# Attention weights and results turned by DVE in 32x32 blocks, with the values' products on 16 TensorE tiles

## The chip, the cores and the metric

The kernel runs on one core of a Trainium2 chip. The metric is the time of one execution on the device, in microseconds (us); lower is better. Five engines run their own instruction streams and meet through semaphores: PE (TensorE), DVE (VectorE), ACT (ScalarE), POOL (GpSimd) and SP, which here only issues DMAs. PE's weight loads are listed apart as PEld.

## The reference

The kernel computes an attention over chunks, and feeds its result to a mixture of experts:

```python
batch, n_heads, seq, head_dim = (4, 8, 768, 64)
chunk, left_ctx, right_ctx = (32, 16, 8)          # and 8 memory keys
for c in range(seq // chunk):
    q_c = q[:, :, c_start:c_end]
    k_full = concat([mem_k, k[:, :, l_start:r_end]], axis=2)
    v_full = concat([mem_v, v[:, :, l_start:r_end]], axis=2)
    scores = scale * q_c @ k_full.T
    scores = scores - max(scores, axis=-1)
    a = exp(scores); a = a / (sum(a, axis=-1) + 1e-09)
    out[:, :, c_start:c_end] = a @ v_full
x = out.transpose(0, 2, 1, 3).reshape(3072, 512)

logits = x @ w_gate; P = exp(logits - logits.max())
for _ in range(8):
    P /= P.sum(1) + 1e-09; P /= P.sum(0) + 1e-09; P *= N / E
out = sum(P[:, e:e+1] * (relu(x @ w1[e]) @ w2[e]) for e in range(8))   # w1: 512x1024, w2: 1024x512
```

All tensors are float32.

## The kernel before, in words

**Tiles.** The 3072 tokens are 24 blocks of 128 queries (four chunks of 32 in a block). A chunk sees a window of 64 keys: 8 of memory, 16 to the left, its own 32 and 8 to the right. Four blocks make a unit of 512 tokens. There are 6 units and 8 experts, 48 pairs of them in all. An expert's two products are done in fp16 parts (a high and a low half, three passes) with a scheme of seven block products in the place of eight (`product`, L1591 to L1598); units 0 and 1 begin with plain products (`first_hidden` L2021, `plain_output` L2110) while their other operands are being made.

**Order.** Each piece of work is a task with an engine, a cost, a due time and its dependencies. A planner, `Plan` (L91), runs a small model of the engines when the kernel is built, and from it writes the order of instructions of each engine by hand. A task on SP or ACT that issues DMAs costs 0.5 us for each issue it is said to have. A task marked `many` (scores and values products) is kept 3.6 us from the last such one. Where PE has nothing to do in the early part, `fill` (L424) puts in products on an idle tile ("warm"). A PE task that writes PSUM takes a bank from a named group, and the task that reads it last gives it back. `Plan.run` takes the bank of the group that has been free longest.

**PSUM before.** There are eight banks of 2 KB for each partition. Group `main` (products of the experts, bank 2 at the start), `early` (banks 0 and 1 of an earlier pool, under number 7, for the scores and values of block 1), `att` (3, 4, 5) and `two` (a tile two banks wide, for scores and values products). When block 1 is through, `hand_over` (L1167) gives banks 0 and 1 to `main`; `lent` (L2206) lends one of `att` to `main`; `turn` (L2221) gives all the rest to `main`, when the attention is over.

**Attention.** `load_block` (L832) and `load_values` (L862) issue the DMAs of q, k and v. `transposed` (L993) turns q and k on PE (tiles tq, tk), `scores` (L1049) makes the weights `s`, 128 queries by 8 heads by 64 keys, and `values` (L1112) ends a block:

1. PE turns the weights with four 128x128 transposes through the identity (`go_t`, L1127, tile ta), and ACT copies them out of PSUM (L1146).
2. PE does 32 products, one for each pair of heads, chunk and head of the pair (`go`, L1137, tile xp): keys of a window (64 rows) by queries of a chunk (32 columns), 65 columns wide, the last of ones for the sum. The profile lists each float32 product as two records, so 64.
3. DVE divides by the sum (`share`, L1155 to L1157).
4. PE turns the result back to features by tokens with four transposes (`go_x`, L1178, tile xt), and ACT copies it to `xg` (L1184).

**Loads of the experts.** `load` (L536) fetches a quarter of w1 (two DMAs of 256 KB, L549) or of w2 (one of 512 KB) on the queue of SP. Pieces called w1fm and w2fm are for the steady part ("m"), w1f and w2f for plain products and for the first units. A maximum over each piece (`most`, L558) leads to a power of two by which `split` (L513, L521) scales it into halves. The gate's weights come by one DMA on SP (L2184), and `logits` (L1388, products at L1399) needs them. A second use of room: v of blocks 4 and on, up to block 6, lies in a buffer that the operands of the experts take later (`x_room`).

## Time and profile before

| | |
|---|---|
| median of 3 runs | 1920.35 us (1920.1 to 1921.62) |
| span of the profiled execution, first to last instruction | 1917.9 us |
| the profiled execution's own time | not listed apart; the span lies 2.45 us below the median of the runs |
| busy: PE, PEld, DVE, ACT, POOL | 1903.2, 1641.0, 1436.4, 1033.6, 524.4 us |
| granted TensorE clock, mean | 1.000 |
| PE transposes of weights (L1127, 96 records) and of results (L1178, 96) | 14.6 and 14.5 us busy |
| values products (L1137, 1536 records in three groups) | 21.2 us busy |

A group of instructions is named by its line, engine, operation, output and inputs. PE's records overlap, as matmuls are pipelined, so that a group's busy time can be longer than the time that it adds; the time from the start of one group to the start of the next is the better measure. "Idle before" is the time in which the engine stood still just before a group, and behind the arrow stands what ended that: an instruction, a DMA, or "issue", for which the profile shows no cause.

### The profile page before, as it was taken

What the parts mean: (1) busy time and instruction counts of PE and PEld (TensorE: products, weight loads), DVE (VectorE), ACT (ScalarE), POOL (GpSimd) and SP (SyncE); (2) the same over time, 40 slices, a digit from 0 to 9 for tenths busy, and PEclk for the clock granted to TensorE, in tenths of its full rate; (3) what the DMA queues carried; (4) which work ended last, traced back from release to release, by engine and by line L of the source; (5) the groups of instructions that cost most, each with busy time, mean ns of one, the idle gap of its engine ahead of it and who ended that gap; (6) DMA issues with size and microseconds to landing.
All of it is one profiled execution on the core that took longest, in us unless ns stands there. A gap on an engine that the chain in (4) does not pass through costs nothing.

```text
span 1917.9 us, 47295 instructions
## 1 busy us (share of the span) xinstructions
PE 1903.2 (99%) x19616; PEld 1641.0 (86%) x19616; DVE 1436.4 (75%) x2396; ACT 1033.6 (54%) x2019; POOL 524.4 (27%) x549
## 2 busy tenths in 40 slices
PE   9999999999999999999999999999999999999999
PEld 7777676688888888888888888888888888888888
DVE  6776569778679866898668875898678885786565
ACT  4765565556456545646445554655555554564453
POOL 1220001544224221432124231342124232332112
PEclk9999999999999999999999999999999999999999
DMA  8678753453235342265214533245313732322321
GB/s 198 174 194 209 171 172 116 129 204 125 83 110 172 127 148 85 78 197 185 92 63 149 197 105 127 78 160 176 138 45 105 242 122 94 100 83 84 127 83 67
DMA packets 246791, 254.82 MB, mean 133 GB/s; under 512 B 113264, under 2 KB 180272, under 8 KB 242224
## 3 DMA queue, kind: packets, MB, share of 16 engines
q1 hardware_dynamic: 244452, 251.21, 41.2%
q8 instruction: 153, 2.51, 0.6%
q10 hardware_dynamic: 2124, 0.59, 0.2%
q14 instruction: 62, 0.51, 0.1%
HBM read 187.84 MB, written 63.44 MB: 131 GB/s over the span
## 4 chain that ended last, share of the span: by engine, by line
PE 96%; DMA 2%; DVE 1%; ACT 0%; issue 0%; SPq 0%; ACTq 0%; DVEq 0%
PE px L1598 26%; PE yx L1598 23%; PE pz L1598 13%; PE yz L1598 11%; PE py L1598 6%; PE yp L2126 6%; PE yy L1598 6%; DMA q<-in_q_dram 1%; PE xp L1137 1%; PE sp L1069 1%; PE pp L2045 1%; PE tq L1006 1%; PE tk L1010 0%; PE ta L1127 0%; PE xt L1178 0%; DVE w L521 0%
## 5 line engine op out<-in xcount | busy, mean ns | idle before, releaser
L1598 PEld LDWEIGHTS <-w 128*128 128x128 f16 x7896 | 771.4, 98 | 91.9 <-issue 0.6
L1598 PEld LDWEIGHTS <-h 128*128 128x128 f16 x7056 | 690.4, 98 | 81.4 <-issue 1.5
L1598 PE MATMUL px<-x,w 128*128 128x256 f16 x4512 | 549.1, 273 | 0.0
L1931 POOL TENSOR_TENSOR acc<-acc,y 128x256 f32<-128x256 f32 x252 | 267.5, 1068 | 862.1 <-ACT y L1906 842.7
L1598 PE MATMUL yx<-w,h 128*128 128x256 f16 x4032 | 467.5, 273 | 1.3 <-DVE acc L1941 1.3
L1657 ACT ACTIVATE q<-px 128x256 f32<-128x256 f32 x376 | 142.8, 381 | 294.2 <-PE px L1598 289.5
L1598 PE MATMUL pz<-x,w 128*128 128x256 f16 x2256 | 278.2, 273 | 0.0
L1598 PE MATMUL yz<-w,h 128*128 128x256 f16 x2016 | 233.8, 273 | 0.0
L1826 DVE TENSOR_TENSOR h<-ss,h 128x1024 f16<-128x1024 f32 x160 | 215.0, 1346 | 4.0 <-ACT h L1802 3.5
L1777 ACT ACTIVATE h<-c 128x768 f16<-128x768 f32 x168 | 140.8, 838 | 106.4 <-DVE c L1667 106.4
L1802 ACT CAST h<-ss 128x1024 f16<-128x1024 f32 x168 | 174.1, 1039 | 20.4 <-DVE ss L1766 19.6
L1766 DVE SCALAR_TENSOR_TENSOR ss<-c,ss 128x256 f32<-128x256 f32 x336 | 168.3, 501 | 8.2
L1810 DVE SCALAR_TENSOR_TENSOR h<-c,h 128x768 f16<-128x768 f32 x168 | 165.3, 984 | 9.2 <-ACT h L1777 9.1
L1667 DVE SCALAR_TENSOR_TENSOR c<-px,q 128x256 f32<-128x256 f32 x188 | 78.0, 422 | 103.2 <-PE px L1598 94.9
L1906 ACT ACTIVATE y<-yx,pscale 128x256 f32<-128x256 f32 x168 | 79.4, 473 | 114.8 <-PE yx L1598 110.6
L1598 PE MATMUL py<-x,w 128*128 128x256 f16 x1128 | 139.2, 273 | 0.0
L2126 PE MATMUL yp<-w,h 128*128 128x512 f16 x576 | 132.0, 379 | 0.0
L1667 DVE SCALAR_TENSOR_TENSOR c<-py,q 128x256 f32<-128x256 f32 x188 | 78.5, 422 | 60.2 <-PE py L1598 56.7
L1766 DVE SCALAR_TENSOR_TENSOR ss<-c,h 128x512 f32<-128x512 f32 x168 | 120.8, 719 | 3.1 <-ACT h L1754 3.0
L1598 PE MATMUL yy<-w,h 128*128 128x256 f16 x1008 | 116.9, 273 | 0.0
L2126 PEld LDWEIGHTS <-h 128*128 128x128 f16 x576 | 56.0, 98 | 57.9
L513 ACT ACTIVATE w<-ws,sw 128x1024 f16<-128x1024 f32 (+1 forms) x64 | 69.3, 1089 | 65.5 <-POOL ws L602 65.5
(158 smaller groups left out, 1773.0 us busy)
## 6 DMA issues: line engine op xcount, KB each, us to landing
x<-xkeep SPq DMA_DIRECT2D x28, 1792.0 KB
akeep<-acc SPq DMA_DIRECT2D x168, 256.0 KB
acc<-akeep SPq DMA_DIRECT2D x168, 256.0 KB
w1f<-in_moe_w_dram SPq DMA_DIRECT2D x72, 256.0 KB
w2f<-in_moe_w_dram SPq DMA_DIRECT2D x32, 512.0 KB
w1fm<-in_moe_w_dram SPq DMA_DIRECT2D x56, 256.0 KB
w2fm<-in_moe_w_dram SPq DMA_DIRECT2D x28, 512.0 KB
xkeep<-x SPq DMA_DIRECT2D x6, 1792.0 KB
```

Source lines behind the costliest of these rows:

```text
L513: lambda: nc.scalar.activation(dst(0), src(), AF.Copy, scale=s),
L1598: nc.tensor.matmul(dst.t, a, b, start=(not more and n == 0), stop=(n == end), skip_group_check=more,)
L1657: lambda: nc.scalar.activation(t.t, src.t, AF.Copy, scale=DOWN),
L1667: lambda: nc.vector.scalar_tensor_tensor(c.t[:, o], src.t, DOWN, q.t, op0=ALU.mult, op1=ALU.add),
L1766: lambda: nc.vector.scalar_tensor_tensor(dst(), src(), 0.0, other(), op0=ALU.max, op1=op),
L1777: lambda: nc.scalar.activation(h.t[:, 0, 0:3], c.t, AF.Relu),
L1802: lambda: nc.scalar.copy(h.t[:, 0, 3:7], ss.t),
L1810: lambda: nc.vector.scalar_tensor_tensor(h.t[:, 1, 0:3].rearrange("p a n -> p (a n)"), c.t.rearrange("p a n -> p (a n)"), 0.0, h.t[:, 0, 0 ...
L1826: lambda: spare.tensor_tensor(h.t[:, 1, 3:7], ss.t, h.t[:, 0, 3:7], op=ALU.subtract),
L1906: (lambda: nc.scalar.activation(t.t, src.t, AF.Copy, scale=f))
L1931: lambda: nc.gpsimd.tensor_tensor(acc.t[:, cols], acc.t[:, cols], q.t, op=ALU.add),
L2126: nc.tensor.matmul(py.t, hf.t[:, hl, where[fh], o : o + P], room(fp, WIDE * wl + DM * fh, WIDE * wl + DM * (fh + 1)), start=(fp == 0 and i ...
```

## The change

The values path of a block becomes: DVE turns the weights in 32x32 blocks (`turn_weights`, one instruction of 128x512), PE does 64 products with 32 keys by 32 queries on the 16 tiles of 32x32 that the array divides into, adding up the two halves of a window (`kh`) in PSUM, DVE divides, and DVE turns the result in 32x32 blocks (`turn_out`, two instructions of 128x256). The four transposes on PE at either side and ACT's two copies are gone. A row group of the array is a chunk and writes into a bank of its own, so that the values products take four adjacent banks (before: two).

Blocks of 32x32 leave the features of x in another order over the partitions: the partition group is the pair `w` of heads, and the four tiles of features are (head of the pair, half of the head). The rows of w1 and of the gate follow that order. So a w1 piece that isn't "m" becomes 8 DMAs of 64 KB (before 2 of 256 KB) and the gate 4 DMAs. v lies with a chunk as a group of 32 partitions and the two halves of its window side by side; the memory rows come by 4 DMAs for a batch element instead of 2 and 2 copies, those of blocks 0 and 1 on ACT's queue.

All of PSUM is one tile, and the planner keeps a time for each bank. A task takes the lowest-numbered bank, or run of adjacent banks, that is free (`room`), where before it took the one that had been free longest. `main` begins with bank 0 and `att` with 1 to 7; `hand_over` gives 1 and 2 to `main`, `lent` gives 3. The planner's cost of the values products (0.9) and the distance of `many` tasks stay.

```diff
+    def room(self, takes, now):
+
+        if takes is None:
+            return now, ()
+        banks = self.free[takes.group]
+        best = None
+        for b in sorted(banks):
+            run = takes.only if takes.only is not None else range(b, b + takes.wide)
+            if all(r in banks for r in run):
+                at = max([now] + [banks[r] for r in run])
+                if best is None or at < best[0]:
+                    best = at, tuple(run)
+        return best
...
-                _, bank = heappop(self.free[t.takes.group])
-                t.takes.bank = bank
-                t.takes.made = t.takes.make(bank)
+                banks = self.room(t.takes, at)[1]
+                for b in banks:
+                    del self.free[t.takes.group][b]
+                t.takes.bank = banks
+                t.takes.made = t.takes.make(banks[0])
...
-                    heappush(self.free[b.group], (b.end, b.bank))
+                    self.free[b.group].update((k, b.end) for k in b.bank)
...
-    plan.free["main"] = [(0.0, 2)]
-    plan.free["early"] = [(0.0, 7)]
-    plan.free["att"] = [(0.0, b) for b in range(3, 6)]
-    plan.free["two"] = [(0.0, 6)]
-
+    plan.free["main"] = {0: 0.0}
+    plan.free["att"] = {b: 0.0 for b in range(1, 8)}
...
+    sums = ps.tile([P, 8, 512], F32, name="sums")
+
+    def bank(group, shape, name, wide=1):
+
+        def view(b):
+            if wide > 1:
+                return sums[:, b : b + wide]
+            size = 1
+            for m in shape[1:]:
+                size *= m
+            t = sums[0 : shape[0], b, 0:size]
+            return t if len(shape) == 2 else t.rearrange("p (a b) -> p a b", b=shape[2])
+
+        return Bank(group, view, wide)
...
+    w1g = w1.rearrange("e (g kt p) (fh fp f) -> e fp g p kt fh f", p=CH, kt=KT, fh=2, fp=FP)
...
-            if which == 1:
+            if which == 1 and ahead == "m":
                 for fh in range(2):
                     queue.dma_start(st.t[:, fh], w1v[e, fp, :, :, fh])
+            elif which == 1:
+                for g in range(CB):
+                    for fh in range(2):
+                        queue.dma_start(
+                            st.t[g * CH : (g + 1) * CH, fh], w1g[e, fp, g, :, :, fh]
+                        )
             else:
                 queue.dma_start(st.t, w2v[e, fp])
 
-        return st, add(eng, 2 if which == 1 else 1, go, after, prio, [st], dma=2.1)
+        return st, add(eng, (2 if ahead == "m" else 6) if which == 1 else 1, go, after, prio, [st], dma=2.1)
...
+            for c in range(CB):
+                p0 = c * CH + WIN - CH
                 queue.dma_start(
-                    vt.t[p0 : p0 + NM, 0, :, 0:D], mem_v[b, par::2].rearrange("h m d -> m h d")
-                )
-
-        def copy_m():
-            for par in range(2):
-                p0 = par * KW + WIN
-                src = vt.t[p0 : p0 + NM, 0:1].rearrange("p c h d -> p c (h d)")
-                queue.dma_start(
-                    vt.t[p0 : p0 + NM, 1:CB].rearrange("p c h d -> p c (h d)"),
-                    src.broadcast_to([NM, CB - 1, HP * DV]),
-                )
-
-        def copy_m0():
-
-            for par in range(2):
-                p0 = par * KW + WIN
-                rows = v_pair[p0 : p0 + NM].rearrange("p n c h d -> p (n c) (h d)")
-                nc.scalar.dma_start(
-                    rows[:, 1:], rows[:, 0:1].broadcast_to([NM, 2 * CB - 1, HP * DV])
+                    vt.t[p0 : p0 + NM, 1, :, 0:D], mem_v[b].rearrange("h m d -> m h d")
...
-        def go_v(pars, queue):
-            for par in pars:
-                p0 = par * KW
+        def go_v(halves_, queue):
+            for kh in halves_:
 
                 def part(c, r, t, m):
-
-                    queue.dma_start(
-                        vt.t[p0 + r : p0 + r + m, c, :, 0:D],
-                        v[b, par::2, t : t + m].rearrange("h t d -> t h d"),
-                    )
+                    p0 = c * CH + r
+                    queue.dma_start(vt.t[p0 : p0 + m, kh, :, 0:D], rows(v, b, t, m))
 
                 for c in range(CB):
+                    t = t0 + c * CH - LC
                     if first and c == 0:
-                        part(0, 0, 0, LC)
-                        part(0, LC, 0, CH + RC)
-                    elif last and c == CB - 1:
-                        part(c, 0, S - CH - LC, CH + LC)
-                        part(c, CH + LC, S - RC, RC)
+                        if kh == 0:
+                            part(c, 0, 0, LC)
+                            part(c, LC, 0, CH - LC)
+                        else:
+                            part(c, 0, CH - LC, WIN - CH)
+                    elif last and c == CB - 1 and kh == 1:
+                        part(c, 0, S - LC, LC)
+                        part(c, LC, S - RC, RC)
                     else:
-                        part(c, 0, t0 + c * CH - LC, WIN)
+                        part(c, 0, t + kh * CH, (CH, WIN - CH)[kh])
...
-            if n == 1:
-                lv.append(vs[0][1][-1])
-            else:
-                eng, queue = ("ACT", nc.scalar) if n == 0 else ("SP", nc.sync)
-                lv.append(add(eng, 2, go_m, (), at - 0.1, [vt], dma=0.1))
-                more = [fill_ones] if n == EARLY - 1 else []
-                copy = copy_m if n > 0 else copy_m0
-                lv.append(add(eng, 2, copy, [lv[-1]] + more, at + 0.1, [vt], dma=0.3))
+            eng, queue = ("ACT", nc.scalar) if n < 2 else ("SP", nc.sync)
+            lv.append(add(eng, 4, go_m, (), at - 0.1, [vt], dma=0.2))
...
-        sp = bank("early" if n == 1 else "two", [P, 2, 512], f"sp_{n}")
+        sp = bank("att", [P, 2, 512], f"sp_{n}", 2)
...
-        aT = buf("at", att, [P, HP, QB], F32, f"at_{n}")
-        tp = bank("att", [P, HP, QB], f"ta_{n}")
-        xp = bank("early" if n == 1 else "two", [P, 2, 512], f"xp_{n}")
-        tx = bank("att", [P, HP, QB], f"xt_{n}")
+        aT = buf("at", att, [P, H, 2, CH], F32, f"at_{n}")
+        xp = bank("att", [P, 4, 512], f"xp_{n}", 4)
         g, o = divmod(n * QB, GT)
         if g not in halves:
             halves[g] = (buf("g", att, [P, KT, GT], F32, f"xg_{g}"), [])
         gt = halves[g][0]
 
-        def go_t():
-            for i in range(HP):
-                nc.tensor.transpose(
-                    tp.t[:, i], s.t[:, 2 * i : 2 * i + 2].rearrange("p h d -> p (h d)"), ident
-                )
+        def turn_weights():
+            nc.vector.transpose(
+                aT.t.rearrange("p h k q -> p (h k q)"), s.t.rearrange("p h k -> p (h k)")
+            )
 
         def go():
-            for i in range(HP):
-                for c in range(CB):
-                    cs = slice(c * CH, (c + 1) * CH)
-                    for par in range(2):
-                        r = slice(par * D, (par + 1) * D)
-                        nc.tensor.matmul(
-                            xp.t[cs, par, i * DV : (i + 1) * DV],
-                            aT.t[r, i, cs],
-                            vt.t[r, c, i],
-                            start=True,
-                            stop=True,
-                        )
-
-        t = add("PE", 0.5, go_t, [made], at, [s, aT], takes=tp)
-        t = add("ACT", 0.6, lambda: nc.scalar.copy(aT.t, tp.t), [t], at, [aT], frees=tp)
+            for a in range(2):
+                for kh in range(2):
+                    for c in range(CB):
+                        r = slice(c * CH, (c + 1) * CH)
+                        for w in range(CB):
+                            nc.tensor.matmul(
+                                xp.t[w * CH : (w + 1) * CH, c, a * DV : (a + 1) * DV],
+                                aT.t[r, 2 * w + a, kh],
+                                vt.t[r, kh, 2 * w + a],
+                                start=(kh == 0),
+                                stop=(kh == 1),
+                            )
+
+        t = add("DVE", 0.62, turn_weights, [made], at, [s, aT])
...
         t = add("PE", 0.9, go, [t] + lv, at + 2, [vt, aT], takes=xp, many=n > 1)
         after_v.append(t)
-        xq = buf("at", att, [P, HP, 2, D], F32, f"xq_{n}")
+        xq = buf("at", att, [P, 2, CB, 2, CH], F32, f"xq_{n}")
         rec = buf("sm", att, [P, H], F32, f"rec_{n}")
 
         def share():
-            x = xp.t[:, :, 0 : HP * DV].rearrange("p a (i d) -> p a i d", d=DV)
-            r = rec.t.rearrange("p (a i) -> p a i", a=2)
+            x = xp.t[:, :, 0 : 2 * DV].rearrange("p c (a d) -> p a c d", d=DV)
...
+            pair = Bank("att", lambda b: None, 2, (1, 2))
+
+            def hand_over():
+
+                pair.group = "main"
+
+            add("-", 0.0, hand_over, [t], -2000.0, takes=pair, frees=pair)
+
+        def turn_out():
+            to = gt.t[:, :, o : o + QB].rearrange("p (a k) (c q) -> p a c k q", a=2, c=CB)
+            for a in range(2):
+                nc.vector.transpose(to[:, a], xq.t[:, a])
+
+        t = add("DVE", 0.72, turn_out, [t], at + 2, [xq, gt])
...
-        lambda: nc.sync.dma_start(
-            gate[:, :, 0:E], w_gate.rearrange("(kt p) e -> p kt e", p=P)
-        ),
+        lambda: [
+            nc.sync.dma_start(
+                gate[g * CH : (g + 1) * CH, :, 0:E],
+                w_gate.rearrange("(g kt p) e -> g p kt e", p=CH, kt=KT)[g],
+            )
+            for g in range(CB)
+        ],
...
-            lent = Bank("att", lambda b: None)
+            lent = Bank("att", lambda b: None, 1, (3,))
...
-                for group in ("att", "two"):
-                    for b in plan.free[group]:
-                        heappush(plan.free["main"], b)
-                    plan.free[group] = []
+                plan.free["main"].update(plan.free["att"])
+                plan.free["att"] = {}
```

More of the change, by code (lines that the diff above doesn't have):

```diff
@@ L80, with __init__ @@
 class Bank:
-    def __init__(self, group, make):
+    def __init__(self, group, make, wide=1, only=None):
         self.group, self.make, self.left, self.end, self.made = group, make, 0, 0.0, None
+        self.wide, self.only = wide, only
     @property
@@ L128, in pad @@
         for banks in self.free.values():
-            if banks and banks[0][0] <= now + 0.2:
-                n = int((at - now - 0.1) * 0.8 / 0.11)
-                if n > 0:
-                    _, bank = heappop(banks)
-                    self.fill(bank, n)
-                    heappush(banks, (now + 0.11 * n + 0.2, bank))
-                return
+            for bank, free in banks.items():
+                if free <= now + 0.2:
+                    n = int((at - now - 0.1) * 0.8 / 0.11)
+                    if n > 0:
+                        self.fill(bank, n)
+                        banks[bank] = now + 0.11 * n + 0.2
+                    return
+    def room(self, takes, now):
[10 more added lines that the diff above has]
+        return best
     def next(self, now, w, a, spread):
@@ L142, in next @@
                 continue
-            if t.takes is None or self.free.get(t.takes.group):
-                at = now
-                if t.takes is not None:
-                    at = max(at, self.free[t.takes.group][0][0])
+            room = self.room(t.takes, now)
+            if room is not None:
+                at = room[0]
                 if pick is None or at < pick[0]:
@@ L155, in next @@
                 break
-            if t.takes is None or self.free.get(t.takes.group):
-                at = r
-                if t.takes is not None:
-                    at = max(at, self.free[t.takes.group][0][0])
+            room = self.room(t.takes, r)
+            if room is not None:
+                at = room[0]
                 if pick is None or at < pick[0]:
@@ L302, in tile_chunked_attn_sinkhorn_moe @@
     ps = ctx.enter_context(tc.tile_pool(name="ps", bufs=1, space=PSUM))
-    pstack = ExitStack()
-    early = pstack.enter_context(tc.tile_pool(name="early", bufs=1, space=PSUM))
     astack = ExitStack()
@@ L413, in sums_buf @@
         )
-    def bank(group, shape, name):
-        return Bank(group, lambda b: banks(b).tile(shape, F32, tag=f"b{b}", name=name))
-    def banks(b):
-        return early if b == 7 else late["ps"] if b < 2 else ps
+    sums = ps.tile([P, 8, 512], F32, name="sums")
[9 more added lines that the diff above has]
+        return Bank(group, view, wide)
     FIRM = 200.0
@@ L424, in fill @@
     def fill(b, n):
-        wp = banks(b).tile([P, 256], F32, tag=f"b{b}", name="warm")
         for _ in range(n):
-            nc.tensor.matmul(wp, idle[:, 0:P], idle, start=True, stop=True)
+            nc.tensor.matmul(sums[:, b, 0:256], idle[:, 0:P], idle, start=True, stop=True)
     plan.fill = fill
@@ L1165, in values @@
         if n == 1:
-            def hand_over(t=t):
-                pstack.close()
-                late["ps"] = ctx.enter_context(tc.tile_pool(name="pl", bufs=1, space=PSUM))
-                del plan.free["early"]
-                for b in range(2):
-                    heappush(plan.free["main"], (t.end + 0.2, b))
-            add("-", 0.0, hand_over, [t], -2000.0, takes=Bank("early", lambda b: None))
-        def go_x():
-            for i in range(HP):
-                nc.tensor.transpose(tx.t[:, i], xq.t[:, i].rearrange("p a d -> p (a d)"), ident)
-        t = add("PE", 0.5, go_x, [t], at + 2, [xq, gt], takes=tx)
-        t = add(
-            "ACT",
-            0.6,
-            lambda: nc.scalar.copy(gt.t[:, :, o : o + QB], tx.t),
-            [t],
-            at + 2,
-            [gt],
-            frees=tx,
-        )
+            pair = Bank("att", lambda b: None, 2, (1, 2))
[7 more added lines that the diff above has]
+        t = add("DVE", 0.72, turn_out, [t], at + 2, [xq, gt])
         halves[g][1].append(t)
```

22 lines of the change are left out of this document (10 added, 12 removed).

## The prediction

> **What bounds the kernel now.** I read the page first, then a table by stage, then the PE timeline around one block's values, then the queue of SP and the chain's steps in the first 110 us.
>
> ```profile
> span 1917.9 us, 47295 instructions
> PE 1903.2 (99%) x19616; PEld 1641.0 (86%) x19616; DVE 1436.4 (75%) x2396; ACT 1033.6 (54%) x2019; POOL 524.4 (27%) x549
> q8 instruction: 153, 2.51, 0.6%
> PE 96%; DMA 2%; DVE 1%; ACT 0%; issue 0%; SPq 0%; ACTq 0%; DVEq 0%
> ```
>
> PE is busy for 99% of the span and holds 96% of the chain that ended last: a microsecond of PE work taken out where PE never runs dry is a microsecond of the end. The table by stage says where that is (columns: the stretch, its length, then busy time and count of PE, PEld, DVE, ACT, POOL, then clock, DMA share and GB/s).
>
> ```profile
> 0.00:34.00 34.00, 30.04 (x470) 24.40 (x471) 17.36 (x36) 14.71 (x26) 4.95 (x12) 1.00 0.82 182
> 34.00:110.00 76.00, 72.71 (x1386) 53.66 (x1387) 59.65 (x102) 54.84 (x108) 19.00 (x24) 1.00 0.73 186
> 110.00:290.00 180.00, 177.07 (x3129) 131.31 (x3128) 113.11 (x222) 102.94 (x214) 14.13 (x19) 1.00 0.71 185
> 290.00:400.00 110.00, 109.96 (x777) 75.60 (x775) 91.41 (x176) 62.66 (x116) 45.15 (x44) 1.00 0.46 152
> ```
>
> The attention lies in the first three stretches. From 110 us on PE is the limit (177.07 of 180, and the clock is 1.00). Before 34 us PE's 30.04 us say little, since most of it is filler; from 34 to 110 us PE is nearly full, but its work arrives by a chain of loads. So the change is two changes: PE work taken out of 16 blocks behind 110 us, and more DMA issues on SP in front of it.
>
> **What the change does on PE.** This is the values path of one block in the steady part (start, length, then the group):
>
> ```profile
> 190.79 0.60 PE L1127 MATMUL ta<-ident,s 128*128 128x128 f32 x4
> 191.23 0.82 PE L1598 MATMUL px<-x,w 128*128 128x256 f16 x6
> 191.88 0.82 PE L1598 MATMUL pz<-x,w 128*128 128x256 f16 x6
> 192.63 0.86 PE L1137 MATMUL xp<-v_pair,at 64*32 64x65 f32 x64
> 193.42 0.83 PE L1598 MATMUL pz<-x,w 128*128 128x256 f16 x6
> ...
> 195.40 0.60 PE L1178 MATMUL xt<-ident,xq 128*128 128x128 f32 x4
> 195.83 0.38 PE L1598 MATMUL pz<-x,w 128*128 128x256 f16 x2
> ```
>
> The lengths overlap, since matmuls are pipelined; what a group costs is its start to the next group's start. The weights' transposes (L1127) cost 191.23 − 190.79 = 0.44 us, the results' (L1178) 195.83 − 195.40 = 0.43, the products (L1137) 193.42 − 192.63 = 0.79. The diff removes both groups of transposes, 0.87 us of PE for each block, and certainly does so: no rival has to be made of that.
>
> The products stay the same in multiplications, but in another shape: 64 records on 8 tiles of 64x32 become 128 records on 16 tiles of 32x32, each tile still working through 4 pairs of records. No row shows 16 tiles. Lower bound: 0.79 us, if the tiles set the time, since each has as many pairs as before. Upper bound: 128 × 0.79/64 = 1.58 us, if each record costs PE's sequencer what it costs now. I take 1.06, a third of the way up: 64 records in 0.79 us leave about 12 ns each, the tiles rather than the issue look like the limit, but the number of records and of weight loads doubles, to 256 PE instructions in one task. So 1.06 − 0.79 = +0.27, and 0.87 − 0.27 = 0.60 us saved in a block. Blocks 8 to 23 lie behind 110 us: 16 × 0.60 = **−9.6 us**. The 4.8 us of blocks 0 to 7 fall where loads set the end, and are counted there.
>
> The Trainium skill's page "TensorE: Matmul & The Clock Gate", section "Part 3: Packing small matmuls", gives a pack of 16 tiles as the time of one matmul plus about 4 ns for each further tile. By it the 128 records need some 0.5 us of issue (an estimate from that page), less than the tiles' 0.79, and the term would be 16 × −0.87 = −13.9; no run here shows 16 tiles.
>
> **What moves to DVE and off ACT.**
>
> ```profile
> L1157 DVE TENSOR_TENSOR xq<-xp,rec 128x512 f32<-128x512 f32 x24 | 16.6, 692 | 2.0
> L1290 DVE TENSOR_TENSOR xt<-xs,xs 128x256 f32<-128x256 f32 x2 | 0.8, 424 | 0.2 <-DMA xs<-gkeep 0.2
> L1146 ACT COPY at<-ta 128x512 f32<-128x512 f32 x24 | 14.0, 584 | 6.5 <-PE ta L1127 6.2
> L1184 ACT COPY xg<-xt 128x512 f32<-128x512 f32 x24 | 14.0, 585 | 21.3 <-PE xt L1178 21.1
> ```
>
> No row shows a DVE transpose. By element operations of the same shapes it is 0.69 for the weights and 2 × 0.42 for the results, 1.53 us a block and 37 us in all; ACT loses 2 × 0.585 = 1.17 a block. DVE is busy 59.65 of 76 and 113.11 of 180, so its 1.53 every 9 us or so is covered by PE's own products: 0. If the transposes took twice that, DVE would still have room in the third stretch; in the first it costs at most 1.5 us, and as little as −1.2 if ACT was what held a block. One block's way from weights to x gets shorter: a turn on DVE and one hop less on either side, 2 × (0.60 + 0.58) − 1.53 − 0.27 = about 0.6 us.
>
> **What moves on SP.** Each of the 36 w1 loads by L549 becomes 8 DMAs of 64 KB instead of 2, and the gate 4 instead of 1.
>
> ```profile
> 15.94 5.81 SPq L549 DMA_DIRECT2D w1f<-in_moe_w_dram  x8
> 24.08 5.50 SPq L921 DMA_DIRECT2D w<-in_v_dram  x8
> 57.79 0.39 SPq L2184 DMA_DIRECT2D gate<-in_moe_w_gate_dram  x1
> 75.70 0.94 SPq L549 DMA_DIRECT2D w1f<-in_moe_w_dram  x2
> ```
>
> The first four pieces take 8 issues and 5.81 us: 0.73 each, more than the 0.39 of a free issue, since the engines' queues are full. With 32 issues of smaller DMAs I take 0.40 each: 12.8 us, +7.0 (bounds: 32 × 0.39 = +6.7, 32 × 0.47 = +9.2, by the later w1 row). Behind them on SP stand q, k and v of the next blocks; the 8 v issues at 24.08 took 0.69 each and can fall to 0.40, as their data has the extra time to drain: 8 × 0.29 = 2.3 back. So SP is +4.7 late at 30 us. The first products need all of it:
>
> ```profile
> 26.36 1.21 DVE L558 TENSOR_REDUCE mxs<-w1f 128x1 f32<-128x1024 f32 x1
> ...
> 32.58 3.67 DVE L521 SCALAR_TENSOR_TENSOR w<-w1f,sw,w 128x1024 f16<-128x1024 f32 x3
> 33.38 1.14 PE L2045 MATMUL pp<-x,w 128*128 128x256 f16 x6
> ```
>
> The maximum over the fourth piece (L558, to 27.57) gives the scale for the split (L521), and the first product starts at 33.38: it comes about 4.7 later, and PE fills with warm products. That in itself is mostly paid by the 4.8 us of PE that blocks 0 to 7 save; what counts is when unit 1's x is there.
>
> ```profile
> 60.28 1.08 PE L1399 MATMUL lp<-xg,gate 128*32 128x128 f32 x32
> 66.71 0.85 PE L1137 MATMUL xp<-x_room,at 64*32 64x65 f32 x64 [0.89 <-DVE lg L1430]
> ...
> 106.47 1.47 PE L1598 MATMUL px<-x,w 128*128 128x256 f16 x12
> ...
> 109.16 1.46 PE L2126 MATMUL yp<-w,h 128*128 128x512 f16 x6
> 110.45 0.82 PE L427 MATMUL warm<-ident 128*128 128x256 bf16 x6
> ```
>
> The gate's issue at 57.79 has all of SP's lateness in front of it and three more issues of 0.39: 4.7 + 1.2 = 5.9. The logits (L1399, 60.28) wait for the gate, block 4's products (66.71) wait for the logits, and unit 1's first product (106.47) for block 7. Less the 0.6 of the shorter block it comes 5.3 later. PE has old work to fill that with: the 6 yp products (110.45 − 109.16 = 1.29), and the 0.66 of filler behind them (to 111.11) goes too. 5.3 − 1.95 = **+3.3 us** (bounds 0, if the early savings let SP's lateness drown, and with 0.47 an issue and nothing regained 9.2 + 1.4 − 2.6 = +8.0).
>
> The second batch of w1 (4 loads between 75 and 99 us, 0.94 for two) grows by 6 × 0.47 = 2.8 each, 11.3 in all, ahead of the q, k and v of blocks 8 and on, which PE needs for unit 2. Those blocks are started well ahead, and each is held apart from the next by the planner's 3.6 us, so most is absorbed: **+1** (bounds 0 and, half of it, +6). The memory rows' DMAs for v change by one or two issues for a batch element: 0.
>
> **What may come as new waits.**
>
> ```profile
> 44.54 0.76 PE L1137 MATMUL xp<-w,at 64*32 64x65 f32 x52
> 46.12 0.34 PE L1137 MATMUL xp<-w,at 64*32 64x65 f32 x12 [0.82 <-issue]
> ...
> 129.39 0.73 PE L1137 MATMUL xp<-v_pair,at 64*32 64x65 f32 x48
> 131.80 0.35 PE L1137 MATMUL xp<-v_pair,at 64*32 64x65 f32 x16 [1.68 <-issue]
> ```
>
> Twice PE stops in the middle of the products for nothing that the profile names, 0.82 and 1.68 us. PE and PEld have 39,232 records and queue 8 carries 153 packets of 16.4 KB (2.51 MB / 153), that is 256 instructions a load: I read the stops as PE running out of code, since a products task is 128 instructions in 0.79 us where 6 big products are 12 in 191.88 − 191.23 = 0.65. A task of 256 is a whole load in about a microsecond, so the stops should grow. Bounds: 0, and one of 1.68 in each of the 16 blocks, 26.9. I take three: **+5.0 us**; against the two of now among 24 blocks of half the size, and below the upper end because matmuls of 0.65/6 = 0.11 us each follow and let the code catch up.
>
> The Trainium skill's "Runtime: NRT & Kernel Launch", section "Instruction fetch mechanics", calls the crossing of such a 16 KiB block mostly hidden. By that rule this term is 0 and the sum 5.0 lower; the two stops above are where this trace disagrees with it.
>
> The last new thing is the choice of PSUM banks: the lowest-numbered free one instead of the one that has been free longest, for every task to the end of the kernel. The planner frees a bank 0.15 us behind its last reader by its own clock; if the real reader is later, PE waits. The chain now shows no such wait, so I have only a small allowance: **+1** (−1, if seven common banks let attention start earlier, to +5).
>
> **Sum.** −9.6 + 3.3 + 1 + 5.0 + 1 = +0.7. The profiled execution's span is 1917.9, 2.45 below the median of the runs shown (1920.35, from 1920.1 to 1921.62); its own whole time isn't listed, so I add the sum to the median: 1921.0 us. About 0.2%, 3.8 us, is what a measurement can tell from no change: 1916.5 to 1924.2.
>
> **Rivals.**
> - A, faster: the 16 tiles cost 0.79 and no code stop comes. −13.9 + 3.3 + 1 + 0 + 1 = −8.6, 1911.7; with the start's loss gone too, 1908.4. For it: four pairs a tile, as now, and only two stops in 24 blocks. Against: those two stops are both in this very task. The two rules above together make this case. Chance 0.30.
> - B, slower by code: stops in half of the 16 blocks, 8 × 1.68 = 13.4 instead of 5.0, 1929.4; in all of them 1942.9. It decides from about 5 stops on (1924.4). For it: queue 8's 256 a load and a task as large. Against: the row 192.63 runs through its 64 without a stop. Chance 0.16.
> - C, slower by issue: products of 1.58, saving 0.87 − 0.79 = 0.08 a block, −1.3 instead of −9.6: 1929.3. It decides from 1.26 us on (a saving lower by 16 × 0.20). Against: 12 ns a record looks like the tiles. Chance 0.08.
> - D, slower by SP: 0.47 an issue, nothing regained, and the second batch at its upper end: +8.0 and +6 instead of 3.3 and 1, 1930.7. Also here: four adjacent banks of four that are left for attention, so that products wait. For it: SP has no pause up to 100 us. Against: PE keeps 72.71 of 76 busy there, so there is work to put first. Chance 0.08.
>
> **How the numbers follow.** The forecast, in which gains and losses cancel, has 0.38, with a range of its own from 1915 to 1928 (the products between 0.79 and 1.26, stops from one to five). Of that, two thirds lie within 0.2%, and the rest falls mostly above. Faster by over 0.2%: A's 0.30 and 0.04 of the forecast. Slower: 0.32 of B, C and D and 0.07. Same: 0.27. The range from 1908 (A with its start) to 1934 (past C and D, B up to ten stops) leaves out about 0.2.
>
> **What would show it.** In the trace after: no L1127 and L1178 transposes, the products of a steady block 1.06 us from start to next start; two DVE transposes' forms near 0.69 and 0.42; SP's first w1 group near 12.8 us; the first product of unit 0 near 38 us and of unit 1 near 111.8; three waits of the products for issue; no wait for a bank behind 400 us. Wrong it is made by products that wait for code in each block, by SP reaching the gate over 8 us late, or by PE falling behind late readers of banks in the long last stage.

## The result and the profile after

The changed kernel takes 1968.64 us (median of 4 runs, 1965.21 to 1971.19) against 1920.98 for the kernel before (1920.10 to 1922.98): 47.7 us slower, ratio 1.0246, 95% interval 1.0232 to 1.0261. Forecast were 1921.0 us and a range that ended at 1934. One of the four executions of run a3 below took 2214.25 us, at a mean granted clock of 0.846 where the others had 0.992 to 0.994, and is left out of a3's median. The changed kernel's page, the stages that were shown of before, and PE's waits from 50 to 400 us:

```profile
span 1963.4 us, 50511 instructions
PE 1924.3 (98%) x21027; PEld 1648.6 (84%) x21027; DVE 1477.9 (75%) x2468; ACT 1008.8 (51%) x1971; POOL 522.4 (27%) x549
q8 instruction: 164, 2.69, 0.5%
PE 88%; DVE 6%; issue 2%; SPq 2%; DMA 2%; POOL 1%; ACT 0%; DVEq 0%; POOLq 0%
```

```profile
0.00:34.00 34.00, 28.48 (x553) 22.35 (x553) 13.11 (x24) 6.74 (x15) 4.95 (x12) 0.95 0.58 122
34.00:110.00 76.00, 66.00 (x1388) 50.46 (x1390) 57.97 (x104) 39.99 (x74) 12.85 (x13) 0.91 0.73 175
110.00:290.00 180.00, 171.14 (x3681) 123.23 (x3657) 127.06 (x246) 86.75 (x182) 17.33 (x24) 0.99 0.65 171
290.00:400.00 110.00, 104.69 (x1329) 72.58 (x1329) 87.19 (x197) 53.32 (x104) 25.63 (x28) 0.97 0.37 124
```

```profile
PE sums L1069 <- issue: 3.8, 2, 2.2
PE sums L1585 <- issue: 2.8, 1, 2.8
PE sums L830 <- DMA kx<-in_k_dram: 2.5, 1, 2.5
PE sums L1521 <- DVE cs L1493: 2.4, 1, 2.4
PE sums L1585 <- DVE c L1654: 2.2, 3, 1.4
PE sums L1134 <- issue: 1.9, 2, 1.1
PE sums L2032 <- issue: 1.2, 1, 1.2
```

PE lost ground in every stage of the attention, and the chain holds 8 points less of PE. (All of PSUM is one tile now, so PE's groups are named by line: L1134 the values products, L1585, L2032 and L2113 the experts' products, L444 filler, L1386 the logits.) The start, from PE, SP and ACT in this order:

```profile
23.41 0.34 PE L1134 MATMUL sums<-v_pair,at 32*32 32x65 f32 x15 [2.11 <-issue]
...
39.16 1.09 PE L1006 MATMUL sums<-ident,q 128*128 128x128 f32 x4 [5.51 <-DMA q<-in_q_dram]
...
50.05 0.82 PE L2032 MATMUL sums<-x,w 128*128 128x256 f16 x6
```

```profile
17.68 17.99 SPq L571 DMA_DIRECT2D w1f<-in_moe_w_dram  x32
35.79 0.38 SPq L872 DMA_DIRECT2D q<-in_q_dram  x1
...
68.75 2.61 SPq L2172 DMA_DIRECT2D gate<-in_moe_w_gate_dram  x4
```

```profile
11.60 1.28 ACT L1034 ACT_TABLE_LOAD   x1 [11.60 <-DMA v_pair<-in_v_dram]
```

The 32 issues of w1 take 17.99 us, 0.56 each, where the forecast had 12.8; q of block 2 stands behind them, PE waits 5.51 us for it, and the first product of unit 0 comes at 50.05 instead of 33.38: 16.7 late, not 4.7. The block in the steady part:

```profile
114.84 1.56 PE L1134 MATMUL sums<-v_pair,at 32*32 32x65 f32 x128
116.33 1.90 PE L2113 MATMUL sums<-w,h 128*128 128x512 f16 x8
```

The products cost 1.49 us (also the median of 22 groups from 50 to 340 us), not 1.06. And the last logits, that is the end of the attention, in the kernel before and the changed one:

```profile
285.58 1.08 PE L1399 MATMUL lp<-xg,gate 128*32 128x128 f32 x32
```

```profile
326.94 1.08 PE L1386 MATMUL sums<-xg,gate 128*32 128x128 f32 x32
```

They are 41.4 us late, which is nearly the 45.5 by which the spans differ. (The experts' products are 36.0 us late behind the routing, and 6 more are lost from 435 to 455 us, in three stops for DVE, the longest of 2.65 us, and a stretch of half clock.) The lateness grows from unit to unit. When the kernel is built the planner has times of its own for the six groups of logits: before 61.1, 98.3, 151.1, 197.7, 248.5 and 287.4, where the chip had them at 60.3, 98.2, 151.8, 198.2, 247.8 and 285.6. For the changed kernel it has 62.5, 97.4, 154.8, 197.5, 249.2 and 286.4; the chip had them at 75.6, 119.0, 180.4, 228.4, 286.4 and 326.9. The old order was written for a chip that behaved as planned to 2 us. The new one spends savings that the chip does not deliver.

PE's time by the start of one matmul to the next, over the whole span, after less before: values path −4.9 us, filler +13.4, gaps above 0.4 us +26.1, the experts' products +8.4 (short gaps and a slow clock in them), the rest +2.9. (A time over 0.4 us from start to start counts as a gap, but for 0.15 us of it.)

The granted clock has a part in this. In the profiled execution of the changed kernel it stood at 0.50 in six stretches of 3.4 to 10.2 us, 30.7 us together; in the kernel before it never did. Each of the six begins during a stop of PE of 2.1 us or more, or at most 1.4 us behind it; the longest stop of the kernel before is 1.68 us. At half clock six products of 128x256 take 1.28 us, where six took 0.65 in the block that the prediction shows:

```profile
107.00 1.48 PE L2032 MATMUL sums<-x,w 128*128 128x256 f16 x6
108.28 1.48 PE L2032 MATMUL sums<-w,w 128*128 128x256 f16 x6
```

So a stop costs more than its gap. An upper estimate is half of the 30.7, 15.4 us; it is less where PE had only filler to do. No run separates this part: it can be in any step of the bill below.

One thing ahead of the prediction has to be corrected: the pieces called w1fm and w2fm are read for their maxima only; w1f and w2f feed all products.

### The profile page after: what moved, and what is told of

It reads as the page before. It is cut to its first block, busy times and chain, and to the rows that moved or that the text cites. A ratio compares the mean times of both kernels' runs of the same rounds, so it can differ in the third digit from the quotient of the medians.

```text
span 1963.4 us, 50511 instructions
## 1 busy us (share of the span) xinstructions
PE 1924.3 (98%) x21027; PEld 1648.6 (84%) x21027; DVE 1477.9 (75%) x2468; ACT 1008.8 (51%) x1971; POOL 522.4 (27%) x549
## 4 chain that ended last, share of the span: by engine, by line
PE 88%; DVE 6%; issue 2%; SPq 2%; DMA 2%; POOL 1%; ACT 0%; DVEq 0%; POOLq 0%
PE sums L1585 79%; PE sums L2113 4%; PE sums L1134 2%; DVE w L538 1%; SPq L571 1%; POOL ws L626 1%; PE sums L2032 1%; PE sums L1069 1%; DVE ss L1753 1%; DVE mxs L582 1%; DMA k<-in_k_dram 1%; PE sums L1006 1%; PE sums L444 1%; DVE x L538 0%; DVE acc L1928 0%
## 5 line engine op out<-in xcount | busy, mean ns | idle before, releaser
L1585 PE MATMUL sums<-x,w 128*128 128x256 f16 x7896 | 880.8, 273 | 7.6 <-DVE c L1654 2.9
L1585 PEld LDWEIGHTS <-w 128*128 128x128 f16 x7896 | 771.8, 98 | 105.0 <-issue 10.9
L1585 PE MATMUL sums<-w,h 128*128 128x256 f16 x7056 | 779.4, 273 | 4.0 <-DVE acc L1928 3.4
L1585 PEld LDWEIGHTS <-h 128*128 128x128 f16 x7056 | 690.6, 98 | 86.2 <-issue 3.8
L1644 ACT ACTIVATE q<-sums 128x256 f32<-128x256 f32 x564 | 214.0, 382 | 357.7 <-PE sums L1585 352.6
L1654 DVE SCALAR_TENSOR_TENSOR c<-sums,q 128x256 f32<-128x256 f32 x564 | 234.3, 422 | 196.1 <-PE sums L1585 183.6
L1893 ACT ACTIVATE y<-sums,pscale 128x256 f32<-128x256 f32 x252 | 118.6, 472 | 147.8 <-PE sums L1585 143.0
L1928 DVE SCALAR_TENSOR_TENSOR acc<-sums,pscale,acc 128x256 f32<-128x256 f32 x252 | 119.4, 478 | 99.3 <-PE sums L1585 73.3
L2113 PE MATMUL sums<-w,h 128*128 128x512 f16 x576 | 132.6, 382 | 0.0
L2113 PEld LDWEIGHTS <-h 128*128 128x128 f16 x576 | 55.8, 99 | 59.6 <-issue 1.1
L538 DVE SCALAR_TENSOR_TENSOR w<-ws,sw,w 128x1024 f16<-128x1024 f32 (+1 forms) x64 | 84.4, 1320 | 23.3 <-ACT w L530 23.3
L626 POOL TENSOR_TENSOR ws<-w1f 128x256 f32<-128x256 f32 x64 | 52.0, 812 | 153.4 <-DVE w L538 95.6
L1732 ACT ACTIVATE h<-sums 128x256 f32<-128x256 f32 x168 | 63.4, 379 | 16.8 <-PE sums L1585 16.3
L1962 DVE SCALAR_TENSOR_TENSOR acc<-sums,pscale,acc 128x256 f32<-128x256 f32 x84 | 39.8, 479 | 37.9 <-PE sums L1585 37.9
```

The source lines that it names most:

```text
L1585: nc.tensor.matmul(dst.t, a, b, start=(not more and n == 0), stop=(n == end), skip_group_check=more,)
L1644: lambda: nc.scalar.activation(t.t, src.t, AF.Copy, scale=DOWN),
L1654: lambda: nc.vector.scalar_tensor_tensor(c.t[:, o], src.t, DOWN, q.t, op0=ALU.mult, op1=ALU.add),
L1893: (lambda: nc.scalar.activation(t.t, src.t, AF.Copy, scale=f))
L1928: lambda: nc.vector.scalar_tensor_tensor(acc.t[:, cols], src.t, f, acc.t[:, cols], op0=ALU.mult, op1=ALU.add),
L2113: nc.tensor.matmul(py.t, hf.t[:, hl, where[fh], o : o + P], room(fp, WIDE * wl + DM * fh, WIDE * wl + DM * (fh + 1)), start=(fp == 0 and i ...
```

## The experiments

Times are medians, ratios are against the kernel before on the same chip, with 95% intervals.

**a1, the w1 and gate DMAs back.** In `load`, and the gate by one DMA:

```diff
-            if which == 1 and ahead == "m":
+            if which == 1:
                 for fh in range(2):
                     queue.dma_start(st.t[:, fh], w1v[e, fp, :, :, fh])
-            elif which == 1:
-                ... 8 DMAs
```

> The changed kernel with w1 pieces in 2 DMAs of 256 KB and the gate in 1 DMA, in the natural order of rows (so the rows don't belong to the features of x: the values are other ones, the work is the same), and the planner's cost of such a load back at 2 issues. Theory S (most of the loss is SP: 32 issues in 17.99 us put the first product 16.7 us late, and nothing wins that back): the first product comes at 33 to 37 us instead of 50, and the time falls by 13 to 20 us from 1968.6, to 1949 to 1956. Rival V (the values products with twice the PE instructions, their code stops and a planner that thinks them cheap make the loss, the start would be absorbed): the time falls by less than 5 us, and the lag of the logits behind the plan at the end of the attention stays near 40 us.

1952.63 us, ratio 1.0169 (1.0147 to 1.0191): 16.0 less than the changed kernel. Theory S holds in its size; but the first product came at 43.9 us, not at 33 to 37, so that a second thing delays the start. V's small gain is refuted, but the last logits were still 30 us behind this kernel's plan (320.1 against 289.7), so what V names is there too. They came only 6.8 us earlier than in the changed kernel, and the two profiled spans differ by 11.2, so not all of the 16.0 went through the end of the attention.

**a2, the same DMAs on the kernel before, alone.** In `load`, 4 groups of 32 partitions by 2, and the gate in 4:

> The kernel before, with its w1 pieces (other than those for maxima) in 8 DMAs of 64 KB, its gate in 4, and the planner's 6 issues for such a load: the part of the change that lies on SP, alone. Theory S: the first product moves from 33.4 to 45 to 50 us, and the time rises by 10 to 18 us from 1921. Rival V: it rises by less than 4 us, as the early part has filler to give.

1940.22 us, ratio 1.0099 (1.0083 to 1.0115): +19.2, a little past S's end.

```profile
16.32 17.34 SPq L554 DMA_DIRECT2D w1f<-in_moe_w_dram  x32
```

```profile
46.42 0.82 PE L2050 MATMUL pp<-x,w 128*128 128x256 f16 x6
```

Here too the group takes over 17 us, and the first product moves by 13.0. The last logits came 19.1 us late, as much as the time rose. From the experiments' two sides, this part costs 16 to 19 us; a1's interval is about 4 us either way.

**a3, the planner's cost of the products.** `add("PE", 0.9, go, ...)` becomes `add("PE", 1.5, go, ...)`:

> The changed kernel with the planner's cost of the values products at 1.5 us instead of 0.9, as the trace shows them (1.49 from start to next start); the instructions of each engine are the same, only their order moves. Theory P (the hand-written order is wrong for the chip because the plan has the products 0.6 us too cheap in each of 24 blocks, so PE waits in order behind things that are late): gaps of PE above 0.4 us shrink from 37.8 us to 25 to 32 us, and the time falls by 5 to 12 us. Rival (order does not matter, the lateness is real work and SP): within 3 us of 1968.6.

1961.19 us, ratio 1.0209 (1.0191 to 1.0227): −7.45 (the expectations further down say 7.3), as theory P had it in time, but not in its sign: PE's gaps were 37.2 us against 37.8. The two profiled spans differ by 4.0 us, mostly less filler (30.9 us against 33.8) and 0.9 in the experts' products, so the mechanism that P names is not shown.

**a4, the choice of bank.** In `room`, for `main` alone:

```diff
-                if best is None or at < best[0]:
-                    best = at, tuple(run)
+                key = at, max(banks[r] for r in run) if takes.group == "main" else b
+                if best is None or key < best[0]:
+                    best = key, tuple(run)
```

> The changed kernel with the old rule of choice for the experts' banks only: among banks that are free at the same time the one that has been free longest, not the lowest-numbered. Theory B (a bank taken again at once makes PE wait for a reader that is later than planned): the lag of the products behind the kernel before, which grows from 42.7 us at 463 us to 45.5 us at the end, stays at 42.7, and some of the waits for DVE at 350 to 450 us go: 3 to 8 us faster than 1968.6. Rival (the banks do not matter, PE is fed by DVE there): within 2 us.

1961.79 us, ratio 1.0212 (1.0194 to 1.0230): −6.9. The two profiled spans differ by 1.8. The products' lag behind the kernel before is 43.3 us at their 3000th record (a 512 wide one counted as two) and 43.7 near the end (changed kernel: 42.7 and 45.5), so about 2.4 us are the late stage that B speaks of. Ahead of it this execution was 0.6 later, not earlier, and its last logits came at 330.7, 3.8 behind those of the changed kernel; where the other 5 us by which the medians differ lie, no trace shows. The late stage is alike in all traces: behind the 3000th record the lag grows by 1.7 to 2.8 us in the six with the lowest-numbered rule (the changed kernel, a1, a3, b1, b3, c3), and by 0.0 to 0.4 in the four with the longest-free one (a4, b5, c1, c7).

**b1, half of the products.** On a1, one half of the window instead of two:

```diff
-                for kh in range(2):
+                for kh in range(1):
```

> As a1_w1_two_dmas (w1 in 2 DMAs, gate in 1, rows in the natural order), and besides the second half of each window is left out of the values products (kh = 0 only): 64 records and 128 PE instructions a block instead of 128 and 256, all else as changed; the values are other ones. Theory C (what is left of the loss in a1, 31.6 us, comes from products that PE pays by the instruction, 1.49 us against the 0.9 that the plan counts, and from stops for code): products of 0.7 to 0.8 us, PE stopped for issue no more than 4 us in all, the last logits 0 to 12 us behind the plan's 289.7 us instead of 30, and a time of 1915 to 1930. Rival (the rest is the start, 10.5 us late in a1 with ACT's longer DMA queue, and DVE's added 37 us): last logits still past 305 us and a time above 1938.

1924.55 us, ratio 1.0024 (1.0015 to 1.0033): 28.1 less than a1, inside theory C's range. The products and the stops:

```profile
200.68 0.86 PE L1128 MATMUL sums<-v_pair,at 32*32 32x65 f32 x64
201.47 1.90 PE L2107 MATMUL sums<-w,h 128*128 128x512 f16 x8
```

```profile
L1128 PE MATMUL sums<-v_pair,at 32*32 32x65 f32 x1216 | 16.7, 226 | 1.4 <-DVE at L1118 0.9 <-issue 0.5
```

0.79 us for 64 records on 16 tiles: the same as for 64 records on 8 tiles before. In a1 PE stood for issue at these lines:

```profile
PE sums L1128 <- issue: 7.1, 4, 3.3
PE sums L1063 <- issue: 2.7, 2, 2.4
PE sums L2026 <- issue: 1.7, 1, 1.7
```

That is 11.5 us, and with 24 × (1.49 − 0.79) = 16.8 for the products makes 28.3, beside the 28.1 measured. Over the whole span the traces split the gain in another way (values path 17.4 us, gaps 5.0, experts' products 3.9, filler 1.9), so the agreement of the two sums is partly luck. The last logits came at 292.3, 2.6 behind the plan and 27.8 earlier than in a1.

```profile
q8 instruction: 152, 2.49, 0.5%
```

That the stops are PE waiting for code is inferred, but from more than the count: they go with the number of instructions, and queue 8 carries 164 loads in the changed kernel and 152 here. Besides, all seven stops for issue in the changed kernel, and all 67 in the fourteen traces of this case, end 1.1 to 1.6 us after a packet of queue 8 has ended, though less than a tenth of the time up to 340 us lies so behind such a packet.

**b3 and b4, narrower products.** 33 columns instead of 65 with the same instructions, on the changed kernel and on the kernel before:

> The changed kernel with values products 33 columns wide instead of 65 (the first 32 features of a head are left out and the others written twice): same 128 records and 256 PE instructions. If the group is bound by issue of instructions, it stays at 1.4 to 1.5 us from start to next start; if by the columns that each tile works through, it falls to 0.75 to 0.95.

> The kernel before with values products 33 columns wide, in the same way: 64 records and 128 PE instructions. If issue bounds it there too, the group stays at 0.75 to 0.79 us; if the tiles bound it, as the prediction had it, it falls to 0.40 to 0.55.

```profile
229.41 1.37 PE L1134 MATMUL sums<-v_pair,at 32*32 32x33 f32 x128
230.71 2.76 PE L2114 MATMUL sums<-w,h 128*128 128x512 f16 x12
```

```profile
193.20 0.76 PE L1137 MATMUL xp<-v_pair,at 64*32 64x33 f32 x64
193.90 0.83 PE L1599 MATMUL pz<-x,w 128*128 128x256 f16 x6
```

1.30 us and 0.70, for half the columns: 0.87 and 0.89 of what they were. Both miss the numbers of either theory by a little, but both are near the count of instructions and far from half. A single execution of each took 1967.86 and 1921.58 us, within 2 us of the medians of the kernels that they were made from. So the group before, too, went by the number of its instructions already. Each product is a matmul and a weight load, and these runs do not say which of the two sets the pace.

**b5, a3 and a4 on a1.**

> As a1_w1_two_dmas, with the planner's cost of the values products at 1.5 us and the longest-free bank for the experts' products (a3 and a4 together, on a1). If these gains are of different places and add up, 1952.6 - 7.3 - 6.9 = 1938 (1934 to 1943). If they are two ways of moving the same order about, the time is 1945 or more.

1945.66 us, ratio 1.0130 (1.0113 to 1.0147): −7.0 where the sum of both would be −14.3. They look mostly like two ways of moving the same order about; the intervals of a1 and b5 (about 4 and 3 us either way) leave room for a part of the sum.

**c4, the transposes alone.** The kernel before with `nc.vector.transpose` in the place of `go_t` and `go_x` and their ACT copies:

> The kernel before with one part of the change alone: DVE's transposes in 32x32 blocks in the place of PE's transposes and ACT's copies, 0.87 us of PE off each block; products on 64x32 tiles, PSUM, loads and their DMAs as before. (Blocks of 32x32 don't give those products their layout: the values are other ones, the work is what this part would cost.) Theory G (PE work taken out is worth its time, as the prediction had it, and DVE has room for the 37 us): first product at 33 to 36 us, last logits 8 to 14 us earlier than 285.6, time 1900 to 1912. Rival (the end of the attention is set by its pace and by DVE, the PE time saved is lost again in the routing): 1916 to 1923.

1916.10 us, ratio 0.9974 (0.9962 to 0.9985): 4 to 5 us faster, at the fast edge of what the rival gave. The values path on PE shrank by 22.2 us, start to start, but filler grew by 5.3 and gaps by 9.9. The last logits were 7.0 early (the plan has them 13.4 early), and the experts' products at most 13.9 ahead of the kernel before, 11.7 at its 308 us; 22 us later they were 3.1 ahead and stayed so. So about half of the 22.2 us was lost ahead of the routing, to filler and to stops such as one of 3.85 us for kx at 88.77, and 8.6 us in it. In the routing, where each of 8 normalisations goes through DVE, PE had run out of other work:

```profile
PE cp L1523 <- DVE cs L1495: 4.9, 2, 3.4
```

```profile
290.00:400.00 110.00, 104.04 (x742) 73.65 (x741) 91.74 (x169) 61.17 (x113) 41.64 (x43) 0.97 0.44 146
```

PE is busy 104.04 of 110 us there, where before it was 109.96, and from 315.9 us on, in the second of its two stops for `cs`, the clock stands at 0.50 for 6.8 us. The transposes themselves are as cheap as estimated:

```profile
L1124 DVE STREAM_TRANSPOSE at<-s 128x512 f32<-128x512 f32 x24 | 16.9, 705 | 1.3 <-ACT s L1108 0.7
L1176 DVE STREAM_TRANSPOSE xg<-xq 128x256 f32<-128x256 f32 x48 | 18.4, 422 | 0.6
```

**c3, ACT's queue; c7, the banks, both on b1.**

> As b1_half_the_products, and the memory rows of v for block 1 are zeros written by POOL, so that ACT has 12 DMA issues ahead of its first table load instead of 16 (block 1's memory values are left out). Theory A (what is left of the late start, first product 38.9 against 33.4 us, hangs on ACT's queue, where the table load begins at 12.0 us instead of 9.1): table load at 10 to 10.5 us, first product 1.5 to 3 us earlier, time 1 to 3 us below 1924.5. Rival (the start hangs on DVE and the order on it): first product within 0.7 us of 38.9.

> As b1_half_the_products, with the longest-free bank for the experts' products. If the lowest-numbered rule costs by itself (a4: 6.9 us, part of it after 460 us), the time falls by 2 to 7 us from 1924.5; if a4's gain came through the early part being late, it is within 1.5 us.

c3: 1922.34 us, ratio 1.0010 (0.9999 to 1.0020). The table load came at 8.98 us (12.41 in b1) and the first product at 36.5, 2.5 earlier, as theory A had it. The gain in time, 2.2, is not clear of noise: its interval overlaps that of b1, and the last logits came at 292.5, no earlier than in b1. c7: 1920.85, ratio 0.9997 (0.9987 to 1.0007), −3.7, clear of b1's interval: the lowest-numbered rule costs by itself.

**c1, mended and complete.** 1.5 for the products, the bank rule of a4, and on the first four pieces `q = nc.gpsimd if g > 1`:

> The changed kernel, complete, with the planner's cost of 1.5 us for the products, the longest-free bank for the experts' products, and half of the w1 issues of the first four pieces on POOL's queue instead of SP's. From a1 (-16.0, all of the 32 issues gone), a3 (-7.3) and b5 (-7.0 for a3 and a4 together): SP's group of 16 takes 8 to 10 us instead of 18, the first product comes at 43 to 46 us, and the time is 1945 to 1956, below the changed kernel and above the one before. If POOL's issues are slow or clog its queue, the first product stays near 50 us and the time is 1957 to 1964.

```profile
16.48 9.26 SPq L573 DMA_DIRECT2D w1f<-in_moe_w_dram  x16
```

1949.36 us, ratio 1.0148 (1.0125 to 1.0171): 19.3 better than the changed kernel. SP's half took 9.26 us; the first product came at 41.0, earlier than expected. It is still 29 us behind the kernel before, and no other complete version came nearer.

**The bill.** Taken apart by single steps: w1 and gate DMAs 16.0 (a1), products and stops 28.1 (b1), banks 3.7 (c7), ACT's queue 2.2 (c3, not clear of noise), transposes −4.1 (c4, by the medians of its runs). Sum 45.9 of 47.7. The steps were measured on different bases, a2 gives 19.2 for the first and a4 6.9 for the third, so the close sum is partly luck.

## Why the prediction was wrong

Term by term, measured against forecast: the products with their stops +28.1 us (b1) for 0.27 × 16 + 5.0 = +9.3; the w1 and gate DMAs +16.0 (a1) for 3.3 + 1 = +4.3; the transposes −4.1 (c4) for 16 × −0.87 = −13.9; the banks +3.7 (c7) for +1; ACT's queue at most +2.2 (c3) for 0. These differences make 45.2 of the 47.0 us by which +47.7 exceeds the forecast's +0.7. The price of the products with their stops is the largest of them.

**"A microsecond of PE work taken out where PE never runs dry is a microsecond of the end."** This is the step that failed first. In c4 22.2 us of PE bought 4 to 5. PE is full until the last logits only because the order fills it with experts' products; those run ahead, and then PE is dry in the routing, which the end of the attention and DVE's sums set. The traces bear this out: in all ten of the changed kernel and its variants the products' lag just behind the routing (at 331 us of the kernel before) is 3.7 to 5.8 us less than that of the last logits, whether that is 3 us (c7) or 45 (a4). c4 itself, made from the kernel before, does not fit this: its lead was 7.0 at the last logits and 3.1 behind the routing, so what sets the routing's end there stays in part open. The stage from 290 to 400 us was quoted as full, 109.96 of 110, and never asked what would fill it when its work had been done early. A stop or a longer group in the attention does count in full, since it delays that end: in b1 the last logits came 27.8 us earlier than in a1, and the time fell by 28.1.

**Products at 1.06 us.** They cost 1.49, near the upper bound of 1.58. "12 ns each, the tiles rather than the issue look like the limit" was the wrong reading: 0.79/64 = 12.3 ns before, 0.79/64 on 16 tiles in b1, 1.49/128 = 11.6 after. It goes by the record, and b3 and b4 show it with narrower products. Rival C, given 0.08, was nearly right in its price a block; it counted 16 blocks. The Trainium skill's rule that the forecast weighed ("TensorE: Matmul & The Clock Gate", "Part 3: Packing small matmuls", about 4 ns a tile) does not hold for this group. The same page of the Trainium skill, in "Back-to-back issue gap", gives a floor of about 25 ns a matmul up to 64 columns; for 64 float32 products that is an estimate of 1.6 us, if one counts the two records of a product as one matmul. The trace's 1.49, at 65 columns, is near it, but b3's 1.30 at 33 columns is 20 ns a product and lies below that floor.

**Code stops, three of 1.68.** The sign was right, the count and the place were not: 9.7 us from 50 to 400 us and one of 2.11 at the start, and b1, with 128 instructions a task, has 0.8 us of them. They strike scores and big products too, up to 9.2 us behind the last values product, not only the products. "Mostly hidden", as the Trainium skill's "Runtime: NRT & Kernel Launch", section "Instruction fetch mechanics", has it, fits most of the changed kernel's 164 loads, but not its seven stops, which take 11.8 us in all.

**SP, 0.40 an issue, +4.7 and +3.3 at unit 1.** An issue took 0.56 (from one start to the next mostly 0.47, three times 1.19 to 1.64), so the group grew by 12.2 instead of 7.0. The forecast had put the 0.73 of before down to full queues; the DMA engines were 0.87 busy then, but only 0.40 from 17.68 to 35.67 us, and an issue still did not take 0.40. Nothing came back: q of block 2 was issued 13.9 later, blocks 2 and on with it (35.79, against this row of before):

```profile
21.87 0.65 SPq L848 DMA_DIRECT2D q<-in_q_dram  x1
```

The forecast set 4.8 us of early PE savings against that, which blocks 0 to 7 did not have (24 blocks saved 4.9 in all). SP reached the gate 11.0 us late, past the 8 that the forecast named as a sign of being wrong, and unit 1's first product came at 128.61, 22.1 late instead of 5.3. The second batch of w1 took 20.85 us on SP instead of 3.82, so it grew by 17.0, not 11.3.

**ACT's queue at 0.** Three more DMAs ahead of its first table load (16 for 13) made it 2.5 us late (before: row below), and PE's first transposes of kx, at 13.55 us, wait 1.28 us for ACT.

```profile
9.14 1.28 ACT L1034 ACT_TABLE_LOAD   x1 [9.14 <-DMA v_pair<-in_v_dram]
```

**Banks +1.** 3.7 to 6.9 by c7 and a4, on either side of the bound of 5; the traces show 1.7 to 2.8 of it, behind 463 us.

**Right** were DVE's prices (0.705 and 0.422 against 0.69 and 0.42) and that the transposes leave PE. Wrong in the way the rivals were used: B, C and D came together, each with a chance of its own under 0.2 and none with the others, though all three push the same thing, the end of the attention, and add up. The four adjacent banks that D also feared are in b1 as well, which is 4.6 us slower than the kernel before, so they cannot cost much.

## What to carry to other kernels

Before crediting time taken off a busy engine, ask what it does next: here about half of the saving went to filler and to waits for loads, most of the rest was lost in a stage that another engine's chain paces, and a fifth was left. Small matmuls on more tiles are not cheaper where the time goes by the instruction; compare the time per record across shapes that are in the trace (12.3 ns for the scores' and the values' 64 alike). In a kernel whose order is written from a plan, put the measured costs of new tasks into the plan first, and compare its times with the trace's: the lag from milestone to milestone shows where the model is wrong.

## What was not expected of the hardware

Splitting a DMA into quarters made the same bytes three times as long to issue: 17.99 us for 32 issues against 5.81 for 8. In the changed kernel stops of PE of 2.1 us and more were followed by half clock in six cases of seven (the 2.76 us that end at 200.62 were not); the longest such stretch goes with the stop of 5.51 us. In the columns of the table by stage, the clock is the third from the right:

```profile
30.00:40.00 10.00, 4.49 (x38) 3.88 (x36) 4.85 (x8) 0.00 (x0) 0.00 (x0) 0.91 0.65 151
40.00:50.00 10.00, 10.00 (x54) 7.34 (x52) 6.68 (x16) 6.97 (x9) 0.00 (x0) 0.58 0.85 136
```

The granted clock was 0.58 from 40 to 50 us, in the very stretch that leads to the first product.
